# Windowed and dilated attention with a mixer block: scores and values in 32-row cells, a masked maximum, a new order of work

## The chip, the cores and the metric

The kernel runs on one core of a Trainium2 chip. The metric is device time in microseconds (us) for one execution: 404.56 us is the median of three runs of the kernel before (403.11 to 404.85). Five engines work side by side, each through its own list of instructions in order: TensorE (PE in the profile, with its weight loads as PEld), VectorE (DVE), ScalarE (ACT), GpSimd (POOL) and SyncE (SP), which here only issues transfers. An instruction waits for semaphores that others raise, and everything behind it on its engine waits too.

## The reference

Eight batches, eight heads, 576 tokens, 64 columns per head. Heads 0 to 3 attend to the last 32 tokens; heads 4 to 7 to every fourth of the last 128 tokens, which is also at most 32 of them. The result goes through a mixer: two matrix products over the tokens, then two over the 512 channels.

```
def _attn_ref(q, k, v):
    B, H, S, D = q.shape
    window, dilation, scale = 32, 4, 1.0 / np.sqrt(D)
    scores = scale * np.matmul(q, k.transpose(0, 1, 3, 2))
    rel = pos[:, None] - pos[None, :]
    mask_plain = (rel >= 0) & (rel < window)
    mask_dil = (rel >= 0) & (rel < window * dilation) & (rel % dilation == 0)
    # heads below H // 2 take mask_plain, the others mask_dil
    scores = np.where(masks[None, :, :, :], scores, -1000000000.0)
    scores = scores - np.max(scores, axis=-1, keepdims=True)
    attn = np.exp(scores)
    attn = attn / (np.sum(attn, axis=-1, keepdims=True) + 1e-09)
    return np.matmul(attn, v)

def _moe_ref(x, w_tok1, w_tok2, w_ch1, w_ch2):
    xt = x.transpose(0, 2, 1)
    h = np.maximum(xt @ w_tok1, 0.0) @ w_tok2
    u = x + h.transpose(0, 2, 1)
    h2 = np.maximum(u @ w_ch1, 0.0) @ w_ch2
    return u + h2
```

## The kernel before

**Tiling.** The 576 tokens stand as five blocks, four of 128 and one of 64. Per batch, q, k and v are loaded as float32 in pieces of one block by all heads (L105: one run of 256 bytes for each head and token) and cast to float16 (L118 on ACT, L121 and L130 on DVE). PE transposes q and k (L190, 40 transposes), DVE copies them out of PSUM (L197, L201).

**Attention, one head at a time.** Scores stand keys by queries: for each of the five key blocks one matrix product of 64 rows gives a cell of 128 keys by up to 256 queries (L143, 5 matmuls a head). ACT takes the exponential of all 1024 columns without a maximum subtracted (L151, L152); a 0/1 mask is multiplied in (L155), on POOL for six heads of eight and on DVE for the others. Since keys stand on the partitions, the result is at once the stationary operand of the product with v (L165, L171, L173, 10 matmuls a head, 128 by 128 times 65 columns, the 65th being ones for the sum). DVE takes the reciprocal (L176) and scales (L179) into `xn`.

**Mixer.** Per batch: `h1p` (L222, 10 matmuls of 512 columns), ReLU on ACT (L229); `up` (L237, 10 of 512) and the sum on DVE (L244); 20 transposes to `uT` (L255, L261) with copies on DVE (L267); `gp`, 96 matmuls of 288 columns (L276), each half of a block's ReLU on ACT (L283) and DVE (L285); `yp`, 60 matmuls of 512 columns, the last 12 of which compute the last 128 tokens again for the sake of 64 (L293, `MST`); sum on DVE (L300) and the store (L302, L304). That is 348 matmuls a batch.

**Order.** `drive` interleaves generators by planned costs: in each round the attention of batch `it` runs beside the mixer of batch `it - 1` and the casts of batch `it + 1`. Loads of batch `it + 2` follow each round. The weights are loaded and cast by transfers from POOL's queue once the first scores exist (`gate`, L340). Six PSUM banks serve all products (`p32`), two the transposes (`tp`).

Of the kernel before, what the change touches and what calls it, by code (L numbers as in the profile page):

```python
# [48 lines left out]

def _np_masks():  # L50
    out = []
    for dil in (False, True):
        m = np.zeros((128, SCW), dtype=np.float16)
        for kb in range(NSB):
            kp = np.arange(128)[:, None]
            qi = np.arange(NQ[kb])[None, :]
            rel = qi - kp
            if dil:
                valid = (rel >= 0) & (rel < WINDOW * DILATION) & (rel % DILATION == 0)
            else:  # L60
                valid = (rel >= 0) & (rel < WINDOW)
            if KW[kb] < 128:
                valid = valid & (kp < KW[kb])
            m[:, COL_OFF[kb]:COL_OFF[kb] + NQ[kb]] = valid.astype(np.float16)
        out.append(m)
    return np.stack(out, axis=0)
# [3 lines left out]
def kernel(  # L70
# [12 lines left out]

# [3 lines left out]
    l32_t = {}  # L87
    q16_t = {}
    k16_t = {}
    vv_t = {}  # L90
    qt_tiles = {}
    kt_tiles = {}
    xn_tiles = {}
    att_hold = {}

    SRC = {"q": q, "k": k, "v": v}

    def emit_loads_dma(b, tensors=("q", "k", "v")):
        for s_i in range(NSB):
            ns = SB[s_i]  # L100
            s0 = 128 * s_i
            for nm in tensors:
                src = SRC[nm]
                t32 = sb.tile([128, H, D], FP32, tag="l32", bufs=15, name=f"l32_{nm}_{b}_{s_i}")
                nc.sync.dma_start(  # L105
                    out=t32[0:ns], in_=src[b, :, s0:s0 + ns, :].rearrange("h s d -> s h d")
                )
                l32_t[(b, s_i, nm)] = t32

    def gen_casts(b):  # L110
        q16 = sb.tile([128, NSB, H, D], FP16, tag="q16", bufs=2, name=f"q16_{b}")
        k16 = sb.tile([128, NSB, H, D], FP16, tag="k16", bufs=2, name=f"k16_{b}")
        vv = sb.tile([128, NSB, H, 65], FP16, tag="vv", bufs=2, name=f"vv_{b}")
        q16_t[b], k16_t[b], vv_t[b] = q16, k16, vv
        for s_i in range(NSB):
            ns = SB[s_i]
            t32 = l32_t.pop((b, s_i, "q"))
            nc.scalar.copy(out=q16[0:ns, s_i], in_=t32[0:ns])  # L118
            yield C_CAST
            t32 = l32_t.pop((b, s_i, "k"))  # L120
            nc.vector.tensor_copy(out=k16[0:ns, s_i], in_=t32[0:ns])  # L121
            if ns < 128:
                nc.vector.memset(k16[ns:128, s_i], 0.0)
            yield C_CAST
            t32 = l32_t.pop((b, s_i, "v"))
            if s_i == 0:
                nc.vector.memset(vv[:, :, :, 64], 1.0)
            if ns < 128:
                nc.vector.memset(vv[ns:128, s_i, :, 0:64], 0.0)
            nc.vector.tensor_copy(out=vv[0:ns, s_i, :, 0:64], in_=t32[0:ns])  # L130
            yield C_CAST

    def emit_qk(b, h):
        hp, r = h // 2, 64 * (h % 2)
        qt = qt_tiles[(b, hp)]
        kt = kt_tiles[(b, hp)]
        scA = ps.tile([128, 512], FP32, tag="p32", bufs=PBUFS, name=f"scA_{b}_{h}")
        scB = ps.tile([128, 512], FP32, tag="p32", bufs=PBUFS, name=f"scB_{b}_{h}")
        for kb in range(NSB):
            q0 = 128 * kb  # L140
            nq = NQ[kb]
            sc, co = (scA, COL_OFF[kb]) if kb < 2 else (scB, COL_OFF[kb] - 512)
            nc.tensor.matmul(  # L143
                out=sc[:, co:co + nq],
                lhsT=kt[r:r + 64, 128 * kb:128 * kb + 128],
                rhs=qt[r:r + 64, q0:q0 + nq],
                start=True, stop=True,
            )
        att = sb.tile([128, SCW], FP16, tag="att", bufs=4, name=f"att_{b}_{h}")
        att_hold[(b, h)] = att  # L150
        nc.scalar.activation(out=att[:, 0:512], in_=scA, func=AF.Exp, scale=0.125)  # L151
        nc.scalar.activation(out=att[:, 512:1024], in_=scB, func=AF.Exp, scale=0.125)  # L152
        m = mask_t[0] if h < 4 else mask_t[1]
        eng = nc.gpsimd if (MASK_ON_POOL[h] and b >= 1) else nc.vector
        eng.tensor_tensor(out=att, in0=att, in1=m, op=ALU.mult)  # L155
        return att

    def emit_av(b, h, att):
        vv = vv_t[b]
        av = ps.tile([128, NSB, 65], FP32, tag="p32", bufs=PBUFS, name=f"av_{b}_{h}")  # L160
        for qb in range(4):
            kbs = [kb for kb in (qb - 1, qb) if kb >= 0]
            for i, kb in enumerate(kbs):
                c0 = COL_OFF[kb] + (0 if kb == qb else 128)
                nc.tensor.matmul(  # L165
                    out=av[:, qb, :],
                    lhsT=att[:, c0:c0 + 128],
                    rhs=vv[:, kb, h, :],
                    start=(i == 0), stop=(i == len(kbs) - 1),
                )  # L170
        nc.tensor.matmul(out=av[:, 4, :], lhsT=att[:, 832:960], rhs=vv[:, 3, h, :],  # L171
                         start=True, stop=False)
        nc.tensor.matmul(out=av[:, 4, :], lhsT=att[:, 896:1024], rhs=vv[:, 4, h, :],  # L173
                         start=False, stop=True)
        rec = sb.tile([128, NSB, 1], FP32, tag="rec", bufs=4, name=f"rec_{b}_{h}")
        nc.vector.reciprocal(out=rec[:, :, 0], in_=av[:, :, 64])  # L176
        xnb = xn_tiles[b]
        a0, a1 = bass.broadcast_tensor_aps(av[:, :, 0:64], rec[:, :, 0:1])
        nc.vector.tensor_tensor(out=xnb[:, :, h, :], in0=a0, in1=a1, op=ALU.mult)  # L179

    def gen_attention(b):
        xn_tiles[b] = sb.tile([128, NSB, H, D], FP16, tag="xn", bufs=2, name=f"xn_{b}")
        q16, k16 = q16_t[b], k16_t[b]
        for nm in ("q", "k"):
            for hp in range(4):
                pst = ps.tile([128, 1024], FP16, tag="tp", bufs=2, name=f"tp_{nm}_{b}_{hp}")
                for s_i in range(NSB):
# [230 lines left out]
```

## Time and profile before

| | |
|---|---|
| three runs | 404.56 us median, 403.11 to 404.85 |
| span of the profiled execution | 403.1 us, all but equal to the fastest run |
| mean granted TensorE clock | 0.962 |
| instructions shown in the profile | 6967 |
| first matmul of the first `gp` | at 48.4 us |
| first `gp` of batches 1 to 7 | at 105.4, 150.9, 194.6, 239.8, 283.6, 327.4 and 372.0 us |

The first `gp` of a batch marks the same point of each round, so the table cuts the span into a start of 48.4 us, a first round of 57.0 us, six rounds of 43.7 to 45.5 us, and an end of 31.1 us. Busy times come from the profiler; matmuls overlap, so that what a matmul costs is read from the distance between two starts, not from its own duration.

### The profile page before, as it was taken

The numbers are of one execution on the slowest core, as the hardware profiler recorded it, in microseconds if no ns is written. First come the engines' busy times: TensorE is split into PE (matmuls) and PEld (weight loads), VectorE is DVE, ScalarE is ACT, GpSimd is POOL, SyncE is SP. The second block draws the span as 40 slices with busy tenths as digits, with TensorE's granted clock in tenths as the row PEclk, the third lists the DMA queues.
The fourth block names the chain that finished last, engine by engine and source line by source line (L and its number), as shares of the span: only waits on it lengthen the run. The fifth ranks groups of instructions, "written<-read, shape, count | busy, mean of one in ns | idle before, by whom it ended". The sixth has DMA issues, their size and how long they took to land.

```text
span 403.1 us, 6967 instructions
## 1 busy us (share of the span) xinstructions
PE 356.7 (89%) x2784; PEld 218.3 (54%) x2784; DVE 228.7 (57%) x550; ACT 137.5 (34%) x281; POOL 101.9 (25%) x69
## 2 busy tenths in 40 slices
PE   0487659997899989999899989998999989996995
PEld 0254337553575547655675557654764557553752
DVE  2487437755885496638754586448543574445432
ACT  2164024443174325422462236331443206321310
POOL 0044301541062404260063205140235106240000
PEclk9999869996899999999899999999999989999899
DMA  9999999349933789486961250020002100020002
GB/s 192 210 214 218 199 198 221 86 112 215 198 77 78 184 180 208 71 210 155 171 122 52 67 91 2 28 78 15 2 0 80 41 0 2 26 80 14 2 38 81
DMA packets 121473, 42.50 MB, mean 105 GB/s; under 512 B 113696, under 2 KB 116064, under 8 KB 121440
## 3 DMA queue, kind: packets, MB, share of 16 engines
q1 hardware_dynamic: 118192, 38.32, 46.3%
q0 software_dynamic: 3248, 3.74, 5.3%
q8 instruction: 22, 0.36, 0.4%
q14 instruction: 11, 0.09, 0.1%
HBM read 36.34 MB, written 9.44 MB: 114 GB/s over the span
## 4 chain that ended last, share of the span: by engine, by line
PE 75%; DVE 13%; DMA 7%; SPq 2%; ACT 1%; issue 1%; POOL 1%; POOLq 0%; ACTq 0%
DMA l_k_3_138<-in_k_dram 6%; SPq L105 2%; DMA l_q_4_83<-in_q_dram 1%; PE yp_4_4709 L293 1%; PE yp_4_4133 L293 1%; PE yp_4_2282 L293 1%; PE yp_4_1665 L293 1%; PE yp_4_3516 L293 1%; PE yp_4_2899 L293 1%; PE yp_3_4669 L293 1%; PE yp_3_4092 L293 1%; PE yp_3_3475 L293 1%; PE yp_3_2241 L293 1%; PE yp_2_918 L293 1%; PE yp_1_877 L293 1%
## 5 line engine op out<-in xcount | busy, mean ns | idle before, releaser
L276 PEld LDWEIGHTS <-w_2_340 128*128 128x128 f16 x192 | 19.5, 102 | 9.9 <-issue 4.7
L276 PEld LDWEIGHTS <-w_0_321 128*128 128x128 f16 x192 | 18.5, 99 | 7.3 <-DVE xn_1159 L179 0.3
L276 PEld LDWEIGHTS <-w_3_357 128*128 128x128 f16 x192 | 19.5, 101 | 5.3
L276 PEld LDWEIGHTS <-w_1_337 128*128 128x128 f16 x192 | 18.9, 101 | 4.2
L190 PE MATMUL tp_q_0_149<-ident,q_0_97 128*128 128x128 f16 (+1 forms) x5 | 1.4, 275 | 14.5 <-ACT q_0_97 L118 14.5
L190 PEld LDWEIGHTS <-q_0_97 128*128 128x128 f16 (+1 forms) x20 | 1.6, 117 | 16.6 <-ACT q_0_97 L118 15.6
L155 POOL TENSOR_TENSOR att_0_792<-att_0_792,mask_63 128x1024 f16<-128x1024 f16 x1 | 2.1, 2116 | 22.0 <-ACT att_0_792 L152 22.0
L155 POOL TENSOR_TENSOR att_0_2548<-att_0_2548,mask_63 128x1024 f16<-128x1024 f16 x1 | 2.1, 2128 | 20.5 <-ACT att_0_2548 L152 20.5
L155 POOL TENSOR_TENSOR att_0_4369<-att_0_4369,mask_63 128x1024 f16<-128x1024 f16 x1 | 2.1, 2120 | 20.5 <-ACT att_0_4369 L152 20.5
L155 POOL TENSOR_TENSOR att_0_1314<-att_0_1314,mask_63 128x1024 f16<-128x1024 f16 x1 | 2.1, 2122 | 19.6 <-ACT att_0_1314 L152 19.6
L155 POOL TENSOR_TENSOR att_0_3165<-att_0_3165,mask_63 128x1024 f16<-128x1024 f16 x1 | 2.1, 2128 | 19.1 <-ACT att_0_3165 L152 19.1
L155 POOL TENSOR_TENSOR att_0_3782<-att_0_3782,mask_63 128x1024 f16<-128x1024 f16 x1 | 2.1, 2124 | 19.1 <-ACT att_0_3782 L152 19.1
L155 POOL TENSOR_TENSOR att_0_1931<-att_0_1931,mask_63 128x1024 f16<-128x1024 f16 x1 | 2.1, 2123 | 19.1 <-ACT att_0_1931 L152 19.1
L346 POOL DMA_DIRECT2D w_0_235<-in_moe_w_tok_dram x1 | 0.7, 720 | 24.5 <-DVE w_1_238 L340 24.5
L237 PEld LDWEIGHTS <-w_0_290 128*128 128x128 f16 x40 | 4.0, 100 | 4.7 <-issue 0.8
L237 PEld LDWEIGHTS <-w_1_304 128*128 128x128 f16 x40 | 3.9, 97 | 3.9
L222 PEld LDWEIGHTS <-w_1_238 128*128 128x128 f16 x16 | 1.7, 105 | 5.9 <-issue 5.2
L276 PE MATMUL gp_0_0_600<-uT_2_589,w_2_340 128*128 128x288 f16 x1 | 0.4, 399 | 4.4 <-DVE uT_2_589 L267 4.4
L155 POOL TENSOR_TENSOR att_4_1535<-att_4_1535,mask_65 128x1024 f16<-128x1024 f16 x1 | 2.1, 2120 | 8.5 <-ACT att_4_1535 L152 8.5
L155 POOL TENSOR_TENSOR att_4_2769<-att_4_2769,mask_65 128x1024 f16<-128x1024 f16 x1 | 2.1, 2123 | 8.2 <-ACT att_4_2769 L152 8.2
L155 POOL TENSOR_TENSOR att_4_4003<-att_4_4003,mask_65 128x1024 f16<-128x1024 f16 x1 | 2.1, 2123 | 8.2 <-ACT att_4_4003 L152 8.2
L155 POOL TENSOR_TENSOR att_4_4585<-att_4_4585,mask_65 128x1024 f16<-128x1024 f16 x1 | 2.1, 2117 | 8.2 <-ACT att_4_4585 L152 8.2
(3217 smaller groups left out, 1288.7 us busy)
## 6 DMA issues: line engine op xcount, KB each, us to landing
w_0_321<-in_moe_w_ch_dram POOLq DMA_DIRECT2D x1, 384.0 KB, 7.8
w_1_337<-in_moe_w_ch_dram POOLq DMA_DIRECT2D x1, 384.0 KB, 9.0
w_2_340<-in_moe_w_ch_dram POOLq DMA_DIRECT2D x1, 384.0 KB, 10.1
w_3_357<-in_moe_w_ch_dram POOLq DMA_DIRECT2D x1, 384.0 KB, 11.1
mask_63<-att_masks SPq DMA_DIRECT2D x1, 256.0 KB, 2.5
mask_65<-att_masks SPq DMA_DIRECT2D x1, 256.0 KB, 3.2
l_q_0_67<-in_q_dram SPq DMA_DIRECT2D x1, 256.0 KB, 3.9
l_k_0_69<-in_k_dram SPq DMA_DIRECT2D x1, 256.0 KB, 4.6
```

The lines of the kernel that those rows point to most:

```text
L105: nc.sync.dma_start(out=t32[0:ns], in_=src[b, :, s0:s0 + ns, :].rearrange("h s d -> s h d"))
L155: eng.tensor_tensor(out=att, in0=att, in1=m, op=ALU.mult)
L190: nc.tensor.transpose(out=pst[:, 128 * s_i:128 * s_i + ns], in_=src[0:ns, s_i, 2 * hp:2 * hp + 2, :].rearrange("s h d -> s (h d)"), identi ...
L222: nc.tensor.matmul(out=p, lhsT=w1[s_i][:, 128 * jb:128 * (jb + 1)], rhs=xnb[:, s_i].rearrange("s h d -> s (h d)"), start=(s_i == 0), stop= ...
L237: nc.tensor.matmul(out=p, lhsT=w2[jb][:, s0:s0 + 128], rhs=h1[jb], start=(jb == 0), stop=(jb == 1),)
L276: nc.tensor.matmul(out=p[:, 0:288], lhsT=w3[cb][:, 128 * mb:128 * (mb + 1)], rhs=uT[cb][:, 288 * sh:288 * (sh + 1)], start=(cb == 0), stop ...
L293: nc.tensor.matmul(out=p, lhsT=gt[mb][:, s0:s0 + 128], rhs=w4[mb], start=(mb == 0), stop=(mb == 11),)
L346: nc.gpsimd.dma_start(out=t, in_=moe_w_tok1[128 * s_i:128 * (s_i + 1), :])
```

## The change

It is a new kernel for the same reference. What it does, in the order of the data:

- q and k are loaded with nine tokens to a partition (`NJ = 9`), so that one run holds 9 x 64 values, 2304 bytes. The transposes (36 a batch) come out in strided order and ACT puts them in place, two copies for each transposed tile. v is loaded three ways: `vp` for the plain heads, `vd` for the dilated ones, and `vs`, a copy of `vp` shifted by 32 partitions.
- Scores stand queries by keys in cells of 32 queries by 64 keys: a stationary operand of 64 rows by 32 columns and 64 moving columns. A query sees at most 32 keys, and 64 keys hold those of 32 neighbours; for the dilated heads the cells take every fourth token. There are 160 such matmuls a batch, alternating between the two halves of the rows (`run_pairs`), in three groups (`qk_run`, 64, 64 and 32).
- The mask is added, a maximum taken over the keys (DVE), subtracted (POOL), the exponential taken (ACT), and 32x32 blocks transposed (DVE).
- Values: 300 matmuls a batch of 32 rows by 32 columns with 65 moving columns, placed on the diagonal of the array (`tile_position`). The dilated heads' result is put back into the order of tokens by transfers within SBUF (`x_perm`, `x_perm4`).
- The last 64 tokens are treated as two column halves of 256, each on 64 partitions (`h1_`, `u_`, `y_mm`): 48 matmuls of 512 columns and 24 of 256 for `yp`, instead of 60 of 512.
- PSUM: three banks for scores and values (`at`), three for the mixer (`mx`), two for transposes.
- The order: each step has a planned time, and the steps are written out in the order of these times.

A batch has 706 matmuls instead of 348. The core of the diff:

```diff
+    def load_qk(n, nm, hq):
...
+                in_=src[n, h0:h0 + 2].rearrange("h (i j) d -> i h (j d)", j=NJ),
...
+    def shift_v(n):
+        s_, d = vp[n % 2], vs[n % 2]
+        nc.sync.dma_start(out=d[32:128], in_=s_[0:96])
+        nc.sync.dma_start(out=d[0:32, 1:5], in_=s_[96:128, 0:4])
...
+    def qk_mm(n, sc, cell, kind, hh, s):
+        par, hp = hh % 2, 2 * kind + hh // 2
+        r0 = 64 * par
+        for g in range(4):
+            if kind == 0:
+                t0 = 128 * s + 32 * g
+                lhs = qT[n % 2][r0:r0 + 64, hp, t0:t0 + 32]
+                rhs = kT[n % 2][r0:r0 + 64, hp, KTO + t0 - 32:KTO + t0 + 32]
...
+            yield dict(out=sc[32 * g:32 * g + 32, cell, :], lhsT=lhs, rhs=rhs, start=True, stop=True)
...
+    def sm_max(n, u, par):
...
+            nc.vector.tensor_tensor(out=s32, in0=sc, in1=mask8, op=ALU.add)
...
+        nc.vector.tensor_reduce(out=mx[:, 0:nc_, 0], in_=s32[:, 0:nc_], op=ALU.max, axis=AX.X)
...
+    def sm_sub(n, u, par):
...
+        nc.gpsimd.tensor_tensor(out=s32[:, 0:nc_], in0=a0, in1=a1, op=ALU.subtract)
...
+        nc.scalar.activation(out=e16[:, 0:nc_], in_=s32[:, 0:nc_], func=AF.Exp, scale=0.125)
...
+        nc.vector.transpose(out=t[:, 0:nc_].rearrange("p c a q -> p (c a q)"),
+                            in_=e16[:, 0:nc_].rearrange("p c j -> p (c j)"))
...
+    def av_run(n, kind):
...
+                        nc.tensor.matmul(
+                            out=av[rows, c - c0, :], lhsT=aT[rows, cell, half, :], rhs=rhs,
+                            start=(half == 1), stop=(half == 0 or skip_prev),
+                            tile_position=(32 * g, 32 * g),
+                        )
...
+    def x_perm(n):
+        xd, x = XD[n], X[n]
+        for r in range(4):
+            nc.sync.dma_start(out=x[r:125 + r:4, 1, 0:16], in_=xd[32 * r:32 * r + 32, 0:16])
...
+    MX = 3
...
+    def m1_(n, mb):
...
+            if sh == 0 or mb % 3 == 2:
+                nc.scalar.activation(out=dst, in_=p[:, 0:288], func=AF.Relu)
+            else:
+                nc.vector.tensor_scalar_max(out=dst, in0=p[:, 0:288], scalar1=0.0)
...
+                for a in range(2):
+                    nc.tensor.matmul(out=p[64 * a:64 * a + 64, 0:256], lhsT=GT[(n, mb)][:, 512:576],
+                                     rhs=w4[:, mb, 256 * a:256 * a + 256],
+                                     start=(mb == 0), stop=(mb == 11))
...
+    at(-1000, init)
+    loads(0, -999)
+    at(-990, gate, 0, ("q", 1))
+    at(-989, wload, 0)
+    for i in range(1, 5):
+        at(-988 + i, wload, i)
+    loads(1, -980)
+    for i in range(5, 9):
+        at(-979 + i, wload, i)
```

Three places show how the instructions now stand.

On PE, in the middle of a round, before: the scores of one head (`scA`, `scB`, two PSUM tiles) between two blocks of `gp`; `kt` is the stationary operand, and the size is that of the result.

```order
L276 MATMUL gp_8_1_3289<-uT_3_3114,w_3_357 128x288
L143 LDWEIGHTS kt_1_3090
L143 MATMUL scA_3_3299<-qt_1_3030,kt_1_3090 128x256
L143 LDWEIGHTS kt_1_3090
L143 MATMUL scA_3_3299<-qt_1_3030,kt_1_3090 128x256
L143 LDWEIGHTS kt_1_3090
L143 MATMUL scB_3_3300<-qt_1_3030,kt_1_3090 128x256
L143 LDWEIGHTS kt_1_3090
L143 MATMUL scB_3_3300<-qt_1_3030,kt_1_3090 128x192
L143 LDWEIGHTS kt_1_3090
L143 MATMUL scB_3_3300<-qt_1_3030,kt_1_3090 128x64
```

Now the first group of scores of a batch begins behind the mixer's transposes, and each matmul gives 32 by 64 values, by turns into the two tiles of the group.

```order
L382 MATMUL tpu_3_2960<-ident,u_2_3_2930 128x128
L212 LDWEIGHTS qT_65
L212 MATMUL sc_0_0_2966<-kT_67,qT_65 32x64
L212 LDWEIGHTS qT_65
L212 MATMUL sc_0_1_2967<-kT_67,qT_65 32x64
```

What was 5 large matmuls between two blocks of `gp` is a run of 64 small pairs of a weight load and a matmul.

On DVE, at the start of `gp` of a batch, before: copies and casts stand between the ReLU instructions (`gt`), and none of them waits for ACT or POOL.

```order
L285 TENSOR_SCALAR gt_0_3124<-gp_0_1_3131 128x288
L201 COPY kt_3_3143<-tp_k_3_3137 128x640
L121 CAST k_7_3913<-l_k_0_3583 128x512
L121 CAST k_7_3913<-l_k_1_3589 128x512
L285 TENSOR_SCALAR gt_1_3145<-gp_1_1_3152 128x288
```

Now the mask's sums (`s`), the maxima (`mx`) and the transposes (`aT`, from ACT's exponentials `e`) of the next batch stand there.

```order
L434 TENSOR_TENSOR o_2_4_4058<-yp_4_4033,u_2_4_2952 128x256
L248 TENSOR_REDUCE mx_0_1_4064<-s_4_0_1_4063 128x8
L407 TENSOR_SCALAR gt_0_4070<-gp_0_1_4077 128x288
L267 STREAM_TRANSPOSE aT_0_0_4149<-e_4_0_0_4067 128x512
L267 STREAM_TRANSPOSE aT_0_1_4170<-e_4_0_1_4151 128x512
L244 TENSOR_TENSOR s_4_1_0_4153<-sc_1_0_4083,mask_62 128x512
L407 TENSOR_SCALAR gt_1_4157<-gp_1_1_4164 128x288
L248 TENSOR_REDUCE mx_1_0_4154<-s_4_1_0_4153 128x8
L244 TENSOR_TENSOR s_4_1_1_4173<-sc_1_1_4084,mask_62 128x512
L248 TENSOR_REDUCE mx_1_1_4174<-s_4_1_1_4173 128x8
L407 TENSOR_SCALAR gt_3_4193<-gp_3_1_4200 128x288
```

The ReLU of `gp_1` stands behind two transposes that wait for exponentials, which wait for POOL, which waits for the maximum some rows ahead.

On POOL, at the start of the program, before: all weights in the order of their use, from the first of `w_tok1` on, behind the gate.

```order
L346 DMA w_0_235<-in_moe_w_tok_dram 128x256
L346 DMA w_1_238<-in_moe_w_tok_dram 128x256
L346 DMA w_2_252<-in_moe_w_tok_dram 128x256
L346 DMA w_3_266<-in_moe_w_tok_dram 128x256
L350 DMA w_4_269<-in_moe_w_tok_dram 64x256
```

Now everything else is issued at once, and the gate (a cast of one value) and the main part of `w_tok1` (L442, tile `w1`) stand last, ahead of the first subtraction (L254).

```order
L443 DMA w1a<-in_moe_w_tok_dram 64x256
L444 DMA w1b<-in_moe_w_tok_dram 64x256
L445 DMA w_77<-in_moe_w_tok_dram 128x2x576
L448 DMA w_78<-in_moe_w_ch_dram 128x4x384 x4
L452 DMA w_79<-in_moe_w_ch_dram 128x3x512 x4
L457 CAST w_74<-lq_1_107 1x1
L442 DMA w_74<-in_moe_w_tok_dram 128x4x256
L254 ISA
L254 TENSOR_TENSOR s_0_0_0_321<-s_0_0_0_321,mx_0_0_322 128x512
```

The weights of the channel products moved ahead of those of the first token product, and all of them ahead of POOL's part in the first softmax.

More of the change, by code (lines that the diff above doesn't have):

```diff
@@ L133, in emit_qk @@
[L133 to L147, printed above, removed]
-            )
[L149 to L179, printed above, removed]
@@ new lines, in at, with one @@
+    def at(t, fn, *a):
+        items.append((t, len(items), fn, a))
+    m8_np, m4_np = _np_masks()
+    ident = sb.tile([128, 128], FP16, tag="ident", name="ident")
+    mask8 = sb.tile([128, 8, 64], FP32, tag="mask8", name="mask8")
+    mask4 = sb.tile([128, 1, 64], FP32, tag="mask4", name="mask4")
+    def one(shape, dt, name):
+        return sb.tile(shape, dt, tag=name, name=name)
+    qT = [one([128, 4, QTW], FP16, f"qT{i}") for i in range(2)]
+    kT = [one([128, 4, KTW], FP16, f"kT{i}") for i in range(2)]
```

671 lines of the change are left out of this document (395 added, 276 removed).

## The prediction

> **What bounds the kernel now.** First the page's busy times and slices, then a table of stretches cut at the first `gp` of a batch, then PE's timeline.
>
> ```profile
> PE 356.7 (89%) x2784; PEld 218.3 (54%) x2784; DVE 228.7 (57%) x550; ACT 137.5 (34%) x281; POOL 101.9 (25%) x69
> ...
> PEclk9999869996899999999899999999999989999899
> DMA  9999999349933789486961250020002100020002
> ...
> q1 hardware_dynamic: 118192, 38.32, 46.3%
> q0 software_dynamic: 3248, 3.74, 5.3%
> q8 instruction: 22, 0.36, 0.4%
> ```
>
> ```profile
> core 0: us, PE busy (x) PEld busy (x) DVE busy (x) ACT busy (x) POOL busy (x), PEclk, DMA share, GB/s
> 0.00:48.40 48.40, 26.40 (x188) 15.31 (x188) 27.01 (x88) 15.45 (x27) 12.57 (x27) 1.00 1.21 207
> 48.40:105.40 57.00, 49.18 (x374) 30.13 (x373) 33.78 (x77) 19.62 (x40) 12.73 (x6) 0.85 0.88 170
> ...
> 239.80:283.60 43.80, 42.00 (x350) 26.01 (x349) 27.04 (x66) 14.37 (x30) 12.73 (x6) 1.00 0.08 28
> ...
> 372.00:403.10 31.10, 26.88 (x162) 16.14 (x161) 9.86 (x19) 4.92 (x12) 0.00 (x0) 0.94 0.11 39
> ```
>
> The start is bound by transfers: 48.4 us at a DMA share above 1, with PE half idle. Then PE binds: a late round is 43.8 us, PE busy for 42.0, DVE for 27, DMA nearly idle. Six rounds from 105.4 to 372.0 take 266.6 us, 44.4 each. So 403.1 = 48.4 + 57.0 + 266.6 + 31.1. The runs' median, 404.56, lies 1.5 above this span and the fastest run, 403.11, on it; I sum against 403.1. About 0.5% is what a measurement of this kernel can tell from no change.
>
> ```profile
> 252.13 0.29 PE L276 MATMUL gp_8_1_3289<-uT_2_3106,w_2_340 128*128 128x288 f16 x1
> 252.25 0.29 PE L276 MATMUL gp_8_1_3289<-uT_3_3114,w_3_357 128*128 128x288 f16 x1
> 252.47 0.39 PE L143 MATMUL scA_3_3299<-qt_1_3030,kt_1_3090 64*128 64x256 f16 x2
> 252.70 0.38 PE L143 MATMUL scB_3_3300<-qt_1_3030,kt_1_3090 64*128 64x256 f16 x3
> 253.01 0.30 PE L276 MATMUL gp_9_0_3311<-uT_0_3082,w_0_321 128*128 128x288 f16 x1
> ...
> 254.98 0.38 PE L165 MATMUL av_1_3337<-vv_2680,att_1_3202 128*128 128x65 f16 x7
> 255.20 0.19 PE L171 MATMUL av_1_3337<-vv_2680,att_1_3202 128*128 128x65 f16 x1
> 255.23 0.19 PE L173 MATMUL av_1_3337<-vv_2680,att_1_3202 128*128 128x65 f16 x1
> 255.26 0.29 PE L276 MATMUL gp_11_0_3351<-uT_0_3082,w_0_321 128*128 128x288 f16 x1
> ...
> 256.24 0.38 PE L293 MATMUL yp_0_3363<-w_0_371,gt_0_3124 128*128 128x512 f16 x1
> 256.46 0.38 PE L293 MATMUL yp_0_3363<-w_1_388,gt_1_3145 128*128 128x512 f16 x1
> ```
>
> Starts give the prices: 0.122 us for 288 columns, 0.216 for 512 (256.24 to 256.46), 0.03 for a 65-column matmul with its weight load. Going into a matmul of 64 rows costs 0.22 instead of 0.12, and coming out 0.31 for 512 columns instead of 0.21: 0.095 each way.
>
> ```profile
> 151.14 0.22 PE L255 MATMUL tpu_2_1866<-ident,u_2_0_1788 128*128 128x128 f16 x1
> 151.19 0.22 PE L255 MATMUL tpu_2_1866<-ident,u_2_1_1801 128*128 128x128 f16 x1
> ```
>
> A transpose is some 0.056.
>
> **A late round after the change, on PE.** `gp` stays: 96 x 0.122 = 11.7 us. `yp`: 48 x 0.216 = 10.4, and 24 of 256 columns, at half of 0.216 each, 2.6, against 60 x 0.216 = 13.0 before; if the two column halves overlap, 1.3. `h1p` and `up`: 16 x 0.216 + 8 x 0.108 = 4.3. Transposes: 54 x 0.056 = 3.0. Seven blocks in small tiles (three groups of scores, two of values, `up` and `yp` of the last tokens), two switches each: 14 x 0.095 = 1.3. That is 33.3 us. What is left is the 460 small pairs, which replace 40 scores and 80 values.
>
> No row shows such a pair. Upper end: 0.03, the 65-column row, if tiles follow one another as full matmuls do (beyond it lies twice that, 0.06, if the weight load isn't hidden either). Lower end: 22 instruction blocks took 0.4% of 16 engines' 403.1 us, 1.2 us each, for 2784 + 2784 instructions, 253 to a block; so instructions cannot come faster than 4.6 ns, 9 ns a pair. Neighbouring pairs stand in different quarters or halves of the array's rows; if those work side by side, a fourth of 0.03 is 7 ns and the instructions bind. I take 12 ns, near the lower end, because each quarter has a row of its own data and the 65-column row is bound by streaming. 460 x 0.012 = 5.5, and the round is 38.8 us.
>
> [...]
>
> **What PE will wait for.** In the stretch from the first group of scores to the dilated values, DVE has, in order:
>
> ```profile
> L285 DVE TENSOR_SCALAR gt_0_599<-gp_0_1_606 x1: 459/459/459, 56.3 to 56.3; 128x288 f16<-128x288 f32 x1
> ...
> L283 ACT ACTIVATE gt_0_599<-gp_0_0_600 x1: 410/410/410, 56.0 to 56.0; 128x288 f16<-128x288 f32 x1
> ...
> L179 DVE TENSOR_TENSOR xn_148<-av_0_273,rec_0_283 x1: 491/491/491, 28.2 to 28.2; 128x320 f16<-128x320 f32 x1
> ...
> L176 DVE RECIPROCAL rec_0_283<-av_0_273 x1: 195/195/195, 28.0 to 28.0; 128x5 f32<-128x5 f32 x1
> ...
> L300 DVE TENSOR_TENSOR o_0_0_860<-yp_0_847,u_0_0_545 x1: 692/692/692, 74.7 to 74.7; 128x512 f32<-128x512 f32 x1
> ...
> L151 ACT ACTIVATE att_0_220<-scA_0_213 x1: 597/597/597, 20.8 to 20.8; 128x512 f16<-128x512 f32 x1
> ...
> L267 DVE COPY uT_0_573<-tpu_0_567 x1: 457/457/457, 47.3 to 47.3; 128x576 f16<-128x576 f16 x1
> ...
> L155 POOL TENSOR_TENSOR att_0_792<-att_0_792,mask_63 128x1024 f16<-128x1024 f16 x1 | 2.1, 2116 | 22.0 <-ACT att_0_792 L152 22.0
> ```
>
> Mask sums are the 512-column sum of 0.69 four times and half of it twice: 3.5. Maxima and block transposes have no row; between the copy's 0.45 and the sum's 0.69 I take 0.6, so 12 of them, four in half size, make 6.0. Six ReLU of 0.46 and two small steps add 3.5: 13.0 us. Twice DVE also stands still for a round trip, because the transposes stand ahead of the next ReLU: POOL's subtraction (half of the 2.1 us row, 1.1, since it has half the columns; between 0.5 and 2.1, as its operands are twice as wide) and ACT's 0.6. That adds some 3.4: 16.4. PE's own work there is 2.6 of `yp`, ten blocks of `gp` (9.8), 96 pairs (1.2) and switches, 14.0. Queued behind the waiting transposes are ReLUs, and with three `mx` banks PE stops two matmul groups later. So PE loses 2.4 us, and a round is **41 us**. Before, six shared banks and no such wait on DVE hid this. The value side costs DVE six times 0.8 (reciprocal and 448 columns at the rate of the 320-column row), beside PE's 13 us of `yp`; `x_perm` has over 5 us of `yp` before `h1p` needs it. ACT has 16 ReLUs, 16 copies of some 0.4, and 3.2 of exponentials, under 20 us; POOL under 24. Neither binds.
>
> **The start.**
>
> ```profile
> l_k_1_73<-in_k_dram SPq DMA_DIRECT2D x1, 256.0 KB, 5.0
> ...
> l_k_3_138<-in_k_dram SPq DMA_DIRECT2D x1, 256.0 KB, 22.7
> ...
> out_dram<-o_0_1_890 SPq DMA_DIRECT2D x1, 256.0 KB, 2.0
> ...
> L155 POOLq EVENT_SEMAPHORE  x40: 17/17/7083, 46.9 to 356.5; - x40
> ```
>
> Loads in 256-byte runs go at 38.32 MB / (46.3% of 403.1 us) = 205 GB/s, 17.2 us for the 3.54 MB of a batch; weights take 5.3% of 403.1, 21.4 us. Stores in 2 KB runs land in 2.0 us against 5.0, so I halve q and k: 2 x 2.9 + 5.8 for v, 11.6 us a batch. When weights run, loads starve (22.7 us for one), so v of batch 0 and the last-issued `w1` arrive together, at about 2 + 11.6 + 21.4 = 35 us. Behind that on SP's queue stand all loads of batch 1 (11.6), and only then the shift copy `vs`: 47 us. POOL's first subtraction is behind the weights too, with a wait of 7.1 us like the one in the last row, done by 45. Then plain values 1.9, scaling 0.8, `h1p` 2.2, ReLU 0.6, `up` 2.2, and 3 for sums, transposes and copies: first `gp` at **58 us**, 9.6 later than now. If loads and weights share better, 50; if the weights' queue stalls POOL longer, 64.
>
> **The first round and the end.**
>
> ```profile
> L276 PE MATMUL gp_0_0_600<-uT_2_589,w_2_340 128*128 128x288 f16 x1 | 0.4, 399 | 4.4 <-DVE uT_2_589 L267 4.4
> ...
> 398.50 0.38 PE L293 MATMUL yp_4_5057<-w_11_487,gt_11_4980 128*128 128x512 f16 x1
> ```
>
> In the first round ACT has 16 ReLUs, 16 copies and six exponentials beside 11.7 us of `gp`, 17 us in all; then `yp` 13, values 3.6, and the next `h1p` to `uT`, 6, with some 3 of waits: **43 us** instead of 57.0, which contained 4.4 us of waiting (the first row) and a mean clock of 0.85. The end: `gp` 11.7, `yp` 13, some stalls, and the 4.6 from the last matmul (the second row) to 403.1: **29**.
>
> Sum: 58 + 43 + 6 x 41 + 29 = **376 us**.
>
> **The rivals.**
>
> Tiles do not overlap (slower). Each pair costs 0.029 as in the 65-column row. PE's round is 33.3 + 13.3 = 46.6, with 0.9 of DVE's wait left: 47.5. Start 60, first round 48: 60 + 48 + 285 + 29 = **422 us**. Against it: the row is bound by its 65 columns through one array, and here four tiles share it. For it: nothing in this trace shows two tiles at work at once. It decides from 20 ns on: a nanosecond a pair is 0.46 us in each of seven rounds and some in the start, 3.4 in all, and 403 - 376 = 27. Chance 0.22; 0.06 for the far end of 0.06 a pair (over 500 us).
>
> Instructions arrive late. A run of values is 288 or 312 instructions, 1.8 us at 12 ns, and a block of 253 takes 1.2 us and its way, 2 us with a store's landing time. Two stops of 1 us a round: 43 us, in all 376 + 7 x 2 = **390**. [...] Chance 0.13.
>
> The waits are smaller. DVE's steps at 0.45, column halves overlapping, pairs at 9 ns: 36 a round, start 54, first round 41, end 28: 54 + 41 + 216 + 28 = **339**. Chance 0.14.
>
> My forecast, 376 with 360 to 390 around it, has 0.45. The range leaves out half of the fast case and most of what lies beyond 430: 340 to 430. Faster: 0.45 + 0.13 + 0.14 less some of the late end, 0.68; within 0.5%, 0.04; slower 0.28.
>
> **What would show it.** Distance of starts inside a group of scores and inside `av`: 12 ns, or 29. First `gp` at 58. Six rounds of 41 by the first `gp` of each batch. Stops of PE before `gp` with DVE's ReLU as releaser, some 2.4 us a round. If POOL's subtraction takes 2 us, or a transfer releases `h1p`, the round is longer for another reason than the pairs, and I am wrong in that step.

## The result, and the profile after

The changed kernel takes **488.77 us** (median of four runs, 487.54 to 490.46) against 403.84 before (four runs, 403.07 to 404.85): 1.212 times as long, 95% interval 1.207 to 1.217. The forecast of 376 us with 340 to 430 around it was wrong, on the sign too. The profiled execution has a span of 488.7 us.

First the page of the changed kernel: busy times, instruction fetches, the chain that ended last (by engine, then by line), and its costliest groups (count, busy us, mean ns, idle before).

```profile
PE 335.7 (69%) x5648; PEld 208.4 (43%) x5648; DVE 205.9 (42%) x437; ACT 256.2 (52%) x337; POOL 111.7 (23%) x142
q8 instruction: 44, 0.72, 0.7%
PE 35%; ACT 32%; DVE 10%; DMA 8%; SPq 6%; POOL 4%; issue 4%; POOLq 0%; DVEq 0%
ACT qT L186 15%; ACT kT L186 14%; PE yp L416 13%; PE gp L400 10%; PE av L300 5%; DMA lvd<-in_v_dram 4%; POOL s L254 4%; DVE mx L248 3%; DVE s L244 3%; ACT e L259 2%; SPq L131 2%; PE tpu L382 2%; DMA lk<-in_k_dram 2%; DMA lq<-in_q_dram 2%; DVE aT L267 1%
L186 ACT COPY qT<-tp_q 128x320 f16<-128x320 f16 (+1 forms) x64 | 86.4, 1714 | 55.8 <-PE tp_q L176 55.8
L186 ACT COPY kT<-tp_k 128x320 f16<-128x320 f16 (+1 forms) x64 | 89.1, 1724 | 2.8 <-PE tp_k L176 2.8
```

PE was busy 89% of the span before and is 69% now, 21 us less in all (335.7 against 356.7). ACT went from 137.5 to 256.2 us and makes 32% of the chain. Nearly all of this share (15% and 14%) is one line: the 128 copies that put transposed q and k into `qT` and `kT`. They keep ACT busy for 175.5 us.

The same cut into stretches as before, at the first `gp` of each batch:

```profile
core 0: us, PE busy (x) PEld busy (x) DVE busy (x) ACT busy (x) POOL busy (x), PEclk, DMA share, GB/s
0.00:79.20 79.20, 20.38 (x538) 13.30 (x539) 26.72 (x66) 26.86 (x27) 23.55 (x34) 1.00 0.87 171
79.20:164.10 84.90, 54.59 (x1103) 33.91 (x1103) 35.88 (x76) 54.68 (x65) 27.39 (x34) 0.76 0.40 98
164.10:209.40 45.30, 38.55 (x413) 23.41 (x412) 14.22 (x30) 29.48 (x37) 8.08 (x10) 0.89 0.42 106
209.40:265.10 55.70, 42.84 (x709) 25.86 (x708) 24.62 (x52) 31.79 (x42) 13.47 (x16) 0.91 0.38 98
265.10:316.00 50.90, 39.69 (x708) 24.81 (x706) 24.71 (x53) 31.77 (x42) 13.35 (x16) 0.97 0.41 102
...
421.40:460.30 38.90, 34.73 (x608) 21.52 (x606) 23.16 (x49) 11.51 (x26) 5.39 (x6) 1.00 0.12 40
460.30:488.70 28.40, 23.74 (x170) 15.25 (x168) 7.28 (x14) 6.56 (x16) 0.00 (x0) 0.95 0.14 47
```

| us | start | first two rounds | five rounds | end | sum |
|---|---|---|---|---|---|
| before | 48.4 | 102.5 | 221.1 | 31.1 | 403.1 |
| forecast | 58 | 84 | 205 | 29 | 376 |
| after | 79.2 | 130.2 | 250.9 | 28.4 | 488.7 |
| after less forecast | +21.2 | +46.2 | +45.9 | -0.6 | +112.7 |

The last round, which has no copies of q and k (no batch follows), takes 38.9 us. It also lacks their 36 transposes, so this alone proves little, but it points at the copies. How they hold the others is seen in the timeline of PE and ACT in a late round (start, duration, group; in brackets the engine's idle time before it and who ended it):

```profile
290.77 5.23 ACT L186 COPY qT<-tp_q 128x320 f16<-128x320 f16 x4 [6.88 <-PE tp_q L176]
...
293.81 0.44 PE L176 MATMUL tp_k<-ident,ck 128*128 128x128 f16 x5 [0.69 <-ACT qT L186]
...
296.06 0.38 PE L176 MATMUL tp_k<-ident,ck 128*128 128x128 f16 x4 [1.81 <-ACT qT L186]
...
296.81 5.23 ACT L186 COPY kT<-tp_k 128x320 f16<-128x320 f16 x4
```

Four copies take 5.23 us: each lasts 1.72 us on average, and the next begins before the last one has ended. There are two `tp` banks, so the third transposed tile waits until ACT has emptied the first, and behind it on PE waits everything else. ACT need not be full for that (31.8 of 50.9 us): PE's order is fixed.

The start, by SP's issue times in the changed kernel (start, time to the end of the group's last issue, line, tile, count):

```profile
38.27 1.75 SPq L134 DMA_DIRECT2D lvd<-in_v_dram  x4
40.06 1.25 SPq L116 DMA_DIRECT2D lq<-in_q_dram  x2
...
53.23 8.04 SPq L131 DMA_DIRECT2D lvd<-in_v_dram  x16
61.31 1.83 SPq L134 DMA_DIRECT2D lvd<-in_v_dram  x4
63.27 0.62 SPq L159 DMA_DIRECT2D vs<-vp  x1
...
64.62 2.45 SPq L324 DMA_DIRECT2D x<-xd  x4
...
68.30 3.68 SPq L329 DMA_DIRECT2D x<-xd  x4
```

SP is done with batch 0 at 40.0 and then issues the 33 loads of batch 1 until 63.1, some 23 us, before it comes to `vs`.

### The profile page after: what moved, and what is told of

The parts are those of the page before. It is cut to its first block, busy times and chain, and to the rows that moved or that the text cites. A ratio compares the mean times of both kernels' runs of the same rounds, so it can differ in the third digit from the quotient of the medians.

```text
span 488.7 us, 13014 instructions
## 1 busy us (share of the span) xinstructions
PE 335.7 (69%) x5648; PEld 208.4 (43%) x5648; DVE 205.9 (42%) x437; ACT 256.2 (52%) x337; POOL 111.7 (23%) x142
## 4 chain that ended last, share of the span: by engine, by line
PE 35%; ACT 32%; DVE 10%; DMA 8%; SPq 6%; POOL 4%; issue 4%; POOLq 0%; DVEq 0%
ACT qT L186 15%; ACT kT L186 14%; PE yp L416 13%; PE gp L400 10%; PE av L300 5%; DMA lvd<-in_v_dram 4%; POOL s L254 4%; DVE mx L248 3%; DVE s L244 3%; ACT e L259 2%; SPq L131 2%; PE tpu L382 2%; DMA lk<-in_k_dram 2%; DMA lq<-in_q_dram 2%; DVE aT L267 1%
## 5 line engine op out<-in xcount | busy, mean ns | idle before, releaser
L400 PE MATMUL gp<-uT,w 128*128 128x288 f16 x768 | 109.1, 292 | 19.9 <-ACT gt L405 13.7
L186 ACT COPY qT<-tp_q 128x320 f16<-128x320 f16 (+1 forms) x64 | 86.4, 1714 | 55.8 <-PE tp_q L176 55.8
L416 PE MATMUL yp<-w,gt 128*128 128x512 f16 x384 | 97.1, 409 | 0.3 <-DVE gt L407 0.3
L400 PEld LDWEIGHTS <-w 128*128 128x128 f16 x768 | 73.8, 99 | 47.6 <-issue 28.0
L186 ACT COPY kT<-tp_k 128x320 f16<-128x320 f16 (+1 forms) x64 | 89.1, 1724 | 2.8 <-PE tp_k L176 2.8
L405 ACT ACTIVATE gt<-gp 128x288 f16<-128x288 f32 x128 | 52.8, 424 | 43.5 <-PE gp L400 39.1
L254 POOL TENSOR_TENSOR s<-s,mx 128x512 f32<-128x512 f32 (+1 forms) x48 | 43.5, 909 | 116.5 <-DVE mx L248 109.3
L416 PEld LDWEIGHTS <-gt 128*128 128x128 f16 x384 | 39.1, 105 | 48.7 <-issue 14.2
L259 ACT ACTIVATE e<-s 128x512 f16<-128x512 f32 (+1 forms) x48 | 27.3, 573 | 46.2 <-POOL s L254 46.2
L300 PEld LDWEIGHTS <-aT 32*32 32x32 f16 x2400 | 24.9, 95 | 48.8 <-issue 31.1
L407 DVE TENSOR_SCALAR gt<-gp 128x288 f16<-128x288 f32 x64 | 28.5, 451 | 35.8 <-PE gp L400 35.2
L267 DVE STREAM_TRANSPOSE aT<-e 128x512 f16<-128x512 f16 (+1 forms) x48 | 29.7, 620 | 18.8 <-ACT e L259 18.7
L300 PE MATMUL av<-vs,aT 32*32 32x65 f16 x608 | 14.2, 197 | 21.6 <-DMA vs<-vp 19.2
```

The lines of the kernel that those rows point to most:

```text
L186: nc.scalar.copy(out=dv[:, :, a], in_=sv[:, :, a])
L254: nc.gpsimd.tensor_tensor(out=s32[:, 0:nc_], in0=a0, in1=a1, op=ALU.subtract)
L259: nc.scalar.activation(out=e16[:, 0:nc_], in_=s32[:, 0:nc_], func=AF.Exp, scale=0.125)
L267: nc.vector.transpose(out=t[:, 0:nc_].rearrange("p c a q -> p (c a q)"), in_=e16[:, 0:nc_].rearrange("p c j -> p (c j)"))
L300: nc.tensor.matmul(out=av[rows, c - c0, :], lhsT=aT[rows, cell, half, :], rhs=rhs, start=(half == 1), stop=(half == 0 or skip_prev), tile_ ...
L400: nc.tensor.matmul(out=p[:, 0:288], lhsT=w3[:, cb, 128 * mb:128 * mb + 128], rhs=UT[n][:, cb, 288 * sh:288 * sh + 288], start=(cb == 0), s ...
```

## The experiments

Each ran beside the kernel before on the same chip, which took 402.3 to 402.8 us. e9 (ten runs) and e12 (four) were repeated, and their runs lie within 3.6 us of each other; the others are single runs, so differences of some 3 us between them mean nothing. Two theories stood at first: (A) the copies are slow because each value is written 18 bytes from the last, and hold PE; (B) SP's row of loads stands ahead of small transfers that PE waits for (the expectation of e4 calls it C, and its rival D). The rival to A was ACT itself, or PSUM as its source; the rival to B was the transfers, which would take their time in any order.

**e1: the copies write side by side.** Tokens then stand in `qT` and `kT` in another order.

```diff
-                nc.scalar.copy(out=dv[:, :, a], in_=sv[:, :, a])
+                nc.scalar.copy(out=flat, in_=sv[:, :, a])
```

> ACT's copies of the transposed q and k write one block behind the other instead of one value every 18 bytes; same count, size and source (the tokens then stand in another order, so the scores are those of other tokens). Theory A, the step of the writes is what makes a copy 1.72 us: copies fall to 0.44 us (187 ns and 0.83 ns a column, from ACT's 288- and 512-column rows), a full round from 51 to 56 us to some 41 (the last round, which has no copies, takes 38.9, and two us of transposes), the first round from 85 to some 52, the start stays near 78, and the whole comes to some 400. Rival B, ACT is slow at reading float16 from PSUM or the copies are not what the rounds wait for: copies stay at 1.7 us, or the rounds stay above 50, and the whole stays within 15 us of 489.

**e2: the same strided copies, on DVE.**

```diff
-                    at(ttr + dtr * i, tr, n, nm, hq, part, nc.scalar)
+                    at(ttr + dtr * i, tr, n, nm, hq, part, nc.vector)
```

> The same strided copies on DVE instead of ACT, result as in the change. If the step of 18 bytes is slow for whoever writes into SBUF: 1.5 to 2 us a copy, DVE's 24.7 us a round become over 50, and the whole stays at 480 to 520. If it is a matter of ACT alone: 0.35 to 0.5 us a copy (DVE's 512-column copy to contiguous places took 0.38 on average), DVE some 32 us a round, rounds of 41 to 44 and a whole of 400 to 420.

**e3: the same result, with the copy's loops turned.** It writes runs of five (or four) neighbours for each of 64 places, and reads PSUM in steps of 256 bytes.

```diff
+            runs = dst[:, hq + 2 * a, o:o + S].rearrange("p (i j) -> p i j", j=NJ)[:, :, j0:j0 + nj]
+            got = sv[:, :, a].rearrange("p j i -> p i j")
-                nc.scalar.copy(out=dv[:, :, a], in_=sv[:, :, a])
+                nc.scalar.copy(out=runs, in_=got)
```

> ACT's copies with the loops turned round: for each of 64 places the five (or four) values that stand next to each other are written in one run of 10 (8) bytes, read from PSUM 256 bytes apart. The result is the change's. Theory A, each separate place that is written costs: a fifth of the places, so 0.5 to 0.8 us a copy, rounds of 41 to 44, a whole of 400 to 420. Rival, every value that is not next to the one before it costs, on whichever side: 1.7 us a copy and 489 as now.

The copies' groups in e1, e2 and e3, in this order:

```profile
L187 ACT COPY kT<-tp_k 128x320 f16<-128x320 f16 (+1 forms) x64 | 21.7, 416 | 15.8 <-PE tp_k L176 15.8
```

```profile
L188 DVE COPY kT<-tp_k 128x320 f16<-128x320 f16 (+1 forms) x64 | 86.6, 1602 | 1.0 <-PE tp_k L176 1.0
```

```profile
L188 ACT COPY kT<-tp_k 128x320 f16<-128x320 f16 (+1 forms) x64 | 24.0, 465 | 12.7 <-PE tp_k L176 12.7
```

e1 took 413.11 us, e2 496.06 and e3 415.28. The step of the writes makes the price: DVE, too, needs 1.6 us, and with a read in steps of 256 bytes (e3) a copy takes 465 ns against 416 in e1. All three copies and the late rounds of e1 and e3 (40.0 to 43.8 us) came out on the side of theory A. e1's total is 13 us above the 400 that it expected, because the first round stayed at 65.2 us where 52 was expected. e3 computes what the changed kernel does and takes back 73.5 of its 488.8 us. Its stretches:

```profile
0.00:80.60 80.60, 21.96 (x539) 14.01 (x540) 26.48 (x66) 12.25 (x27) 23.09 (x34) 1.00 0.87 176
80.60:145.80 65.20, 48.52 (x1104) 31.38 (x1103) 35.93 (x76) 25.24 (x65) 27.47 (x34) 0.84 0.47 119
145.80:179.20 33.40, 33.30 (x414) 21.81 (x413) 14.13 (x30) 14.70 (x37) 8.09 (x10) 1.00 0.55 143
...
223.00:263.50 40.50, 37.35 (x709) 24.26 (x708) 24.58 (x52) 17.04 (x42) 13.43 (x16) 1.00 0.50 123
```

The five late rounds are 205.9 us (43.8, 40.5, 42.4, 40.5, 38.7); the forecast had 205. With the copies turned, a full round is only 2 to 5 us longer than the last one; in the changed kernel it was 12 to 17. The start is as bad as before the repair (80.6), and the first two rounds, 98.6, are still 14.6 over the forecast's.

**e4: in the changed kernel, the loads of batch 1 behind `vs`.**

```diff
-    loads(1, -980)
+    loads(1, 7.6)
```

> Only the loads of batch 1 move behind the shifted copy of v on SP's queue. Theory C, the start of 79.2 us (58 forecast) is SP's own time to issue 33 loads ahead of that copy, 23 us: the first gp comes at 58 to 62, and the whole falls by 10 to 19 us, less what batch 1 then waits for its loads. Rival D, the start is set by the weights that starve the loads of batch 0, or by POOL: the first gp stays above 75 and the whole within 5 us of 489.

It took 489.34 us, first `gp` at 77.7. These are the rival's numbers, but they don't decide: `vs` went out at 39, and `x_perm` still stood behind the 33 loads:

```profile
39.09 0.62 SPq L159 DMA_DIRECT2D vs<-vp  x1
...
61.25 1.84 SPq L134 DMA_DIRECT2D lvd<-in_v_dram  x4
63.18 2.45 SPq L324 DMA_DIRECT2D x<-xd  x4
```

The next four, on e3's copies, move one thing each in the start.

**e5: batch 1's loads behind batch 0's `x_perm4`. e6: e5 with v of batch 0 issued by ACT. e7: e5 with a hold on the weights. e8: e6 and e7.**

```diff
# e5
-    loads(1, -980)
+    loads(1, 25.3)
# e6, in load_v
+        dq = nc.scalar if n == 0 else nc.sync
# e7, ahead of wload(1)
+        nc.gpsimd.tensor_copy(out=w3[96:97, 0, 0:1], in_=L[(n, "vd")][96:97, 4, 0, 0:1])
```

> The copies of e3 (runs of five), and batch 1's 33 loads issued on SP behind batch 0's x_perm4, not ahead of vs. Theory (SP's issue time is what holds x_perm of batch 0 back): vs is copied at about 39 and x_perm at about 50 to 54, not at 65 to 72; the first gp product comes at 58 to 64 in place of 80.6, the first round takes longer than the 65.2 plus 33.4 of e3's first two together by no more than 10 (batch 1 arrives later), time 393 to 405. Rival A (the transfers, not SP's issue, set the start: batch 0, the weights and batch 1 have to come in anyway): first gp at 75 or later, or as much lost in the first two rounds as won, time 412 to 418. Rival B (the late x_perm is due to the values' instructions coming late to TensorE): first gp at 70 to 77.

> e5 with the 25 loads of v of batch 0 issued by ACT, not by SP. If SP's issue time (0.43 to 0.62 us a DMA) sets when batch 0's last v load is out, the casts of v start 6 to 12 us earlier than in e5 and so does the first gp product, time 385 to 398; if the transfers do it (v shares the DMA engines with the weights), first gp within 3 us of e5.

> e5 with the transfers of w3 and w4 held until batch 0's last v load has landed (a copy of one value on GpSimd ahead of them). If the weights' transfers starve v in the start (3.1 MB beside 3.5 MB of batch 0), v is in by 22 to 28 in place of 38, the first gp product comes at 45 to 52, time 382 to 395. If SP's issue time does it, v comes no earlier than in e5 and the weights come later: first gp 0 to 10 later than in e5.

> e6 and e7 together. If each of issue time and transfers holds v back in turn, this is the fastest: first gp at 42 to 48, time 378 to 390; if only one of them counts, as the better of e6 and e7 within 3 us.

| us | time | first `gp` | first two rounds | third round begins |
|---|---|---|---|---|
| e3 | 415.28 | 80.6 | 98.6 | 179.2 |
| e5 | 408.28 | 59.2 | 112.8 | 172.0 |
| e6 | 406.67 | 72.4 | 98.7 | 171.1 |
| e7 | 407.97 | 60.0 | 112.9 | 172.9 |
| e8 | 408.25 | 70.7 | 99.6 | 170.3 |

e5 brought the first `gp` forward by 21.4 us, as theory B said for the start, and lost 14.2 of it in the first round: neither side's total. e6 missed: with v on a second queue the last cast of q and k, which SP still loads, came at 31.4 (17.2 in e5), and the first `gp` at 72.4. e7 held back only the one part of the weights that its copy touches; the other parts were issued ahead of it, at 3 to 9 us, so it says nothing on the weights, and e8, which joins the two, no more. What the table does say is that in e5 to e8 the third round begins at 170 to 173 wherever the start lies. Something later held it.

**e9: every part of `w3` and `w4` held until v of batch 0 is in (eight such copies), and `vs` and `x_perm` of batch 0 issued by ACT. e10: the hold alone, on e5. e11: ACT's issue alone, on e3.**

```diff
# shift_v, x_perm, x_perm4
+        dq = nc.scalar if n == 0 else nc.sync
-        nc.sync.dma_start(out=d[32:128], in_=s_[0:96])
+        dq.dma_start(out=d[32:128], in_=s_[0:96])
...
```

> Copies of e3; every transfer of w3 and w4 held until batch 0's last v load is in (eight copies of one value on GpSimd, one into each part), and batch 0's vs and x_perm issued by ACT, so that SP's order no longer holds them; batch 1's loads where the changed kernel has them. Theory (in the start 3.1 MB of weights and SP's row of loads stand ahead of batch 0's values, and this is all of the difference that is left): v of batch 0 in by 24 to 28 in place of 38, first gp product at 44 to 52, the first two rounds together as e3's (98.6) within 5, time 378 to 390, faster than the kernel before by 3 to 6%. Rival (v is slow of itself, 25 transfers in rows of 256 bytes): v in at 33 or later, first gp at 55 or later, time 392 to 402.

> The same hold on the weights, with vs and x_perm on SP and batch 1's loads behind x_perm as in e5. By the theory first gp at 46 to 54 here too, but the first two rounds together stay as in e5 (112.8), since batch 1 still comes late: time 392 to 400. By the rival (v slow of itself) first gp at 59 or later, time 405 or more.

> e3 with vs and x_perm of batch 0 issued by ACT and nothing else moved. If only their place on SP behind batch 1's loads held them, first gp comes at 58 to 64 as in e5 and, with batch 1's loads as early as in e3, the first two rounds stay near 98.6: time 392 to 400. If the transfers of batch 1 hold batch 0's small transfers and TensorE's instructions back (as they seemed to in e4), first gp at 66 or later, time 400 to 413.

e9 took 405.3 us, 1.007 (1.004 to 1.010) of the kernel before; first `gp` at 53.3, third round at 169.1. e10: 406.96, 52.2 and 168.7. e11: 407.29, 62.6 and 169.1. So both parts of the start are right: the hold on the weights brings 7 to 9 us (e10 against e5, e9 against e11), and ACT's issue 18 (e11 against e3). In e11 the loads of batch 1 go out as early as in e3, so it is their place ahead of `vs` and `x_perm` that cost these 18 us, not their transfers. The totals are all missed, mainly because the first two rounds took 115.8, 116.5 and 106.5 us, against 98.6 in e3. SP's timeline in e9, in the first round, shows why it may be so there:

```profile
90.57 1.83 SPq L134 DMA_DIRECT2D lvd<-in_v_dram  x4
92.50 0.61 SPq L161 DMA_DIRECT2D vs<-vp  x1
...
118.16 1.83 SPq L134 DMA_DIRECT2D lvd<-in_v_dram  x4
120.09 0.84 SPq L437 DMA_DIRECT2D out_dram<-o  x2
120.99 2.45 SPq L329 DMA_DIRECT2D x<-xd  x4
```

`vs` of batch 1 waits behind the loads of batch 2, and `x_perm` of batch 1 behind the loads of batch 3, which end at 120. That would be the fault of the start once more, and e12 tests it.

**e12: e9 with `vs` and `x_perm` of batches 0, 1 and 2 issued by ACT. e15: the same without the hold on the weights. e14: the changed kernel with its own copies, and only these transfers moved.**

```diff
-        dq = nc.scalar if n == 0 else nc.sync
+        dq = nc.scalar if n < 3 else nc.sync
```

> e9 with vs and x_perm of batches 0, 1 and 2 issued by ACT. In e9 the first two rounds took 115.8: SP issued vs of batch 1 at 92.5, behind the 33 loads of batch 2, and x_perm of batch 1 at 121.0, behind the 33 loads of batch 3. Theory (SP's order is what makes the first two rounds long): first gp at 53 as in e9, the third round begins at 142 to 152 in place of 169.1, time 376 to 388, faster than the kernel before by 3.5 to 6.5%. Rival (the transfers of batches 1 to 3 set these rounds, whoever issues them): third round begins at 162 or later, time 397 or more.

> The same without the hold on the weights: copies of e3, and vs and x_perm of batches 0, 1 and 2 on ACT's queue. Theory: first gp at 62 to 63 as in e11, then as in e12, time 384 to 398, so that the hold on the weights is worth 7 to 10. Rival: third round begins at 165 or later, time 402 or more.

> The changed kernel with its own copies (steps of nine values), and only vs and x_perm of batches 0, 1 and 2 moved to ACT's queue. If the two causes add up, first gp at 60 to 64 in place of 79.2, and the first two rounds (130.2) come down by 10 to 25 but not below two of its later rounds (some 104), time 445 to 468. If with the slow copies SP's order costs nothing of its own in these rounds, only the start comes down: 468 to 474.

| us | time | first `gp` | first two rounds | five rounds | end |
|---|---|---|---|---|---|
| e12 | 393.35 | 54.8 | 97.7 | 212.0 | 28.0 |
| e15 | 397.52 | 63.2 | 93.7 | 210.8 | 28.0 |
| e14 | 479.00 | 63.1 | 127.3 | 258.8 | 28.0 |

In e12 the third round begins at 152.5, against 169.1 in e9. That is theory B's side, half a microsecond past its bound and far from the rival's 162. Its total of 376 to 388 was missed: at 393.35 us (four runs, 391.46 to 395.0) e12 is 0.978 (0.972 to 0.983) of the kernel before, so the changed kernel, with its copies turned, its weights held back and its queue put right for three batches, is a little faster than the kernel before, by some 2% and not by the 3.5 to 6.5% expected. In the profile of e12:

```profile
54.80:109.70 54.90, 45.80 (x889) 30.19 (x889) 25.64 (x54) 22.90 (x60) 18.51 (x25) 0.94 0.58 134
109.70:152.50 42.80, 38.69 (x628) 24.22 (x626) 25.92 (x55) 17.56 (x43) 15.84 (x20) 0.96 0.58 146
152.50:199.40 46.90, 41.40 (x709) 25.48 (x707) 24.69 (x51) 17.15 (x42) 16.67 (x20) 0.93 0.58 142
```

e15 (one run) lies at the upper end of its expectation: the hold on the weights is worth 8.4 us in the first `gp` and some 4 in the time, not 7 to 10. e14 came out over both of its expectations: with slow copies the start gains 16 us, the first two rounds 3, and the late rounds give 8 back. In its four full late rounds PE waits 39.5 us for the copies, against 31.2 in the changed kernel, which is the 8 us. ACT's issue of transfers can't be the reason there: the last one that ACT issues in e14 goes out at 159 us, and from then on SP issues them all, as in the changed kernel. Why PE waits longer stays open.

Moving the transfers has a price on ACT, which works in its own order and now stands before `x_perm` until the values are there. Its group of copies in e12 shows it:

```profile
L190 ACT COPY qT<-tp_q 128x320 f16<-128x320 f16 (+1 forms) x64 | 23.6, 459 | 70.9 <-PE tp_q L178 55.2 <-DMA x<-xd 10.6 <-POOL vp L156 4.6
```

Before these copies ACT idles 10.6 us for the transfer of `x` and 4.6 for the cast of `vp`; in e3 it idles there for PE alone. A third queue for these transfers was not tried.

## Why the prediction was wrong

**The step that failed first: "ACT has 16 ReLUs, 16 copies of some 0.4 ... Neither binds."** I took the copy's price from a DVE row that writes side by side (457 ns). The diff writes `dst` with nine values from one to the next, and no row of before showed such a write. Measured: 1.72 us each (0.41 in e1, side by side, and 0.46 in e3, in runs of four or five), four in a row 5.23 us, 21.9 us of ACT a batch against some 6. The mechanism that I left out (PE's fixed order behind two `tp` banks) then made a round 50.9 us where e3 has 40.5; in those two rounds PE waits 8.1 and 0 us for these copies. I gave no bound from the other side for this one operation, so no rival held it. This is 45 of the 113 us in the five rounds, and 31.6 more in the first two (130.2 against 98.6).

**The second: "all loads of batch 1 (11.6)".** I used the time that the transfers take. What stands ahead of `vs` is SP's time to issue 33 of them, 23.1 us. Some 20 of these are the issuing instructions themselves, and the 33 loads of a later batch, spread over a late round, still take 17.4 to 17.9 us of SP's time: it is in the main a cost per load, 0.61 us on average there and 0.53 to 0.54 in the late rounds. The 11.5 us that the sum lacks here are over half of the 21.2 by which the start was late. Five more are the loads of batch 0 (40.0, not 35), and five the steps behind `vs` (15.9, not 11), where `x_perm` was left out of the sum. e5 and e11 show the cause: with the loads out of the way the first `gp` comes at 59.2 and 62.6, against the 58 forecast. In e14, the changed kernel with nothing but these transfers moved, it comes at 63.1.

**The third: the first round of 43 us** counted one batch of copies and one of attention. The planned times put the casts, transposes and scores of batch 2 into it as well (1103 matmuls, and 413 in the second round), so only the two rounds together can be held against 84. They were 130.2; the copies make 31.6 of the excess of 46.2, and 14.6 are left in e3. SP's order counts here too: between e9 and e12, which start alike (53.3 and 54.8), only its place for batches 1 and 2 differs, and the two rounds go from 115.8 to 97.7. That is more than the 14.6 of e3; that e3's late start gave the loads more time is a reading that was not tested apart. With the order put right 10 (e15) to 14 us (e12) over the forecast remain. In e12 PE is busy for 84.5 us of these two rounds (45.8 and 38.7) and idle for the other 13, so PE's work alone fills the forecast's 84. A small part of it is work of batch 3: 36 transposes and 64 scores more than two rounds hold, some 2.5 us. The rest stays open: no wait of PE in these rounds is large enough alone; the longest is 4.1 us, for a copy that stands on ACT behind the issue of `vs`.

**What was right.** The small pairs are cheap, and tiles overlap. The timeline of the values in a late round of the changed kernel (four matmuls to a line):

```profile
283.42 0.20 PE L300 MATMUL av<-vs,aT 32*32 32x65 f16 x4
283.45 0.20 PE L300 MATMUL av<-vp,aT 32*32 32x65 f16 x4
283.48 0.20 PE L300 MATMUL av<-vs,aT 32*32 32x65 f16 x4
283.51 0.20 PE L300 MATMUL av<-vp,aT 32*32 32x65 f16 x4
```

Twelve starts in 0.09 us are 7.5 ns each; a whole run of 144 takes 1.21 us from the first start to the last, 8.5 ns each, where a 65-column matmul of the kernel before took 0.03 us. Scores come faster still at first: of 64 in a row in a late round, the first 32 start 4.0 ns apart and the other 32, after a pause of 0.1 us, 8.3 ns. I had 12 ns, an estimate between two bounds, and no run tests the reasons that I gave for it. The lower end of 9 ns a pair, which I took from the instruction blocks, was no floor. So the rival "tiles do not overlap", which was to end on the slow side, is refuted, and the kernel is slower for a reason that none of the rivals named.

"Instructions arrive late" is there, but small. In the five late rounds PE loses 2.1, 0.2, 2.9, 0.3 and 1.8 us with "issue" as the releaser, that is, waiting for nothing that the profile shows; most of it stands before values. That is 1.5 us a round where the rival had 2, and e3 has the same 1.5. The profile's page counts 44 instruction blocks against 22 before, but no run ties the stops to them. They are longer in the start, where the DMA share is 0.87 in the changed kernel against 0.41 in its round from 265.10 on: in e4 PE stops inside the values for 2.06 and 5.83 us, which no run explains further.

With e3's copies the sum's other terms stand: rounds of 41.2 on average over the five (forecast 41; the four full ones average 41.8), an end of 28.4 (29). In part that is luck. A full round of e3 has 1 us less of PE's work than the 38.8 forecast, in line with the cheaper pairs, and some 4 us of waits instead of 2.4. Nor was DVE's ReLU the main one to wait for, as forecast: PE waits 0.9 us a round for it and 1.4 to 1.9 for ACT's. The round trip was right, but it holds ACT's ReLU as well, behind an exponential that waits for POOL. In a late round of e3:

```profile
226.25 0.63 ACT L261 ACTIVATE e<-s 128x512 f16<-128x512 f32 x1 [1.11 <-POOL s L256]
226.79 0.69 ACT L407 ACTIVATE gt<-gp 128x288 f16<-128x288 f32 x2
...
227.24 0.65 PE L402 MATMUL gp<-uT,w 128*128 128x288 f16 x4 [0.83 <-ACT gt L407]
```

## What to carry to other kernels

Price a copy by the step of its writes, not by its count of values (here 1.72 us against 0.41 for as many values side by side): where the trace has no row with that step, bound it by several times the contiguous row (here it was four times) and ask who waits for it in a fixed order. A row of loads on a queue delays what stands behind it by its issue time, here some 20 us for 33 loads; small transfers inside SBUF that the next matmul needs belong on another queue (in e11 the first `gp` came 18 us sooner than in e3), at a price for the engine that issues them (in e12 ACT idled 10.6 and 4.6 us for it). And when the start is repaired, look for the same row of loads ahead of the next batch before counting the gain: here the third round began at 152.5 with the order put right for three batches (e12), against 169.1 for one (e9).

## What was not expected of the hardware

A copy of 320 values a partition in 18-byte steps took 1820 to 1876 ns and one of 256 values 1573 to 1609: 4.0 ns for each further value, against 0.55 in e1 (429 to 434, and 394 to 399). In e3 both shapes took 461 to 466: both have 64 runs, of five or four values, so the time went with the count of runs and not of values.

The issue of one 32 KB load on SP took 0.43 us (e9 from 83 us on). In the start of the changed kernel 16 of them were spread over 18.96 us, of which only 7.9 were issuing; between them SP waited for earlier loads to land (7.0 us for `lvp`, 3.7 for `lvd`).

In e9's first round the granted clock was low in a stretch in which PE had little to do:

```profile
90.00:100.00 10.00, 3.19 (x174) 2.66 (x172) 3.42 (x8) 1.12 (x4) 2.57 (x5) 0.61 0.68 188
100.00:110.00 10.00, 3.11 (x154) 2.13 (x153) 7.71 (x14) 2.40 (x4) 6.90 (x7) 0.50 0.98 216
```

PE was busy for a third of these 20 us, and the clock was 0.50 to 0.61. But in the same run from 20 to 30 us PE was busy for 1.38 us at 1.00, so what lowered the clock was not worked out. What the matmuls did at such a clock shows in the changed kernel: from 90 to 100 us, at 0.51, those of `gp` mostly start 240 ns apart, against 123 from 79.2 to 90, at 1.00.
